# Due times that follow from the next holder of a buffer, a shift by one tensor_reduce, and another order of a split, in a planned attention and MoE kernel on one core

## The chip, the core and the metric

The kernel runs on one core of a Trainium2 chip. Its engines work side by side, each through its own instructions in the order written: TensorE (PE, with PEld for its weight loads), VectorE (DVE), ScalarE (ACT), GpSimd (POOL), and SyncE (SP), which here only issues DMAs. PE writes into PSUM, of which there are 8 banks; DVE and ACT read it, POOL works in SBUF alone. The metric is the device time of one launch in microseconds; less is better.

## The reference

Per batch of 8 and head of 8, with 576 positions and 64 channels, the attention is linear: keys and queries go through an exponential feature map with 128 features. Its output is the input of a dense layer pair (512 to 2048 to 512) with a gate between.

```python
def phi(x):                                   # x scaled by 64 ** -0.25
    proj = np.einsum('bhsd,md->bhsm', x, omega)
    sq = np.sum(x * x, axis=-1, keepdims=True) / 2.0
    h = proj - sq
    h = h - np.max(h, axis=-1, keepdims=True)
    return np.exp(h) / np.sqrt(m)
...
kv = np.einsum('bhsm,bhsd->bhmd', k_p, v)
z = np.sum(k_p, axis=2)
num = np.einsum('bhsm,bhmd->bhsd', q_p, kv)
den = np.einsum('bhsm,bhm->bhs', q_p, z)[..., None] + 1e-06
x = num / den                                 # then (batch, position, head * 64 + channel)
...
h = x @ w_in
sp = np.maximum(h, 0.0) + np.log1p(np.exp(-np.abs(h)))
out = (h * erf(sp)) @ w_out
```

## The kernel before

**Precision.** The large products are made in a fast reduced-precision float form (fp32r). Each operand is split into a high part (a rounded copy) and a low part (the difference), and a product is three matmuls: high by high, high by low, low by high. So a copy ("xhigh", "turnhigh", "high") and a subtraction ("xrest", "turnrest", "rest") stand in front of nearly every matmul.

**Attention.** Two heads make a pair; there are 32 pairs, 4 to a batch (NP). Pairs 0 to 3 (batch 0) go through one by one at the start (`first`, `project_pair`). From pair 4 on, two pairs make a quad (`load`, `project`, `attention`), 14 of them, two to a batch. For keys and for queries of a quad, `project` makes three projections; each fills two PSUM banks (tiles pp), one a pair. For each bank DVE takes the negated maximum over the features (`maximum`, into mx), then `shift` adds the squares, and ACT takes exponentials with that as bias (`exponential`, into f). The squares come from a second layout of q and k (tile un): squared on POOL or ACT, halved twice by POOL additions (`fold`, from 64 to 16 columns a position), and summed by DVE (`sum_squares`, into sq). `shift` runs two scalar_tensor_tensor over the same 6 elements a partition: the squares times half_sq are added to mx and then taken away again, so that mx carries the rounding that the reference has (sq is the same for all features, so it falls out of the exponential but for that rounding). Then `key_values` multiplies exponentials of the keys with v, `turn` transposes those of the queries through PSUM (tiles pt, parts qh and ql), `attend` multiplies both (tiles nd), and a reciprocal and a multiplication on DVE give xs.

**The dense layers.** A batch is 576 positions, two halves of 288. The first layer is done by phase: two phases (ph) a batch, each with 4 granules (fp) of two 128-row blocks. In batches 0 to 2 (PLAIN = 3) a granule is eight plain products (tiles h); from batch 3 on it is seven products of sums and differences of blocks (tiles hS, hA), which takes one product out of eight. Their results are copied or added into hs (names hout and hadd), `chain` runs softplus and erf on ACT for two granules at a time (the activation tables are loaded for it), then the gate (hs times gs, on DVE or POOL), a rounded copy gh and the rest gl. The second layer (`gemm2`, tiles o) of the phase before is done between the granules of this one. Weights are unpacked once in the first two batches by integer operations (wshift, wsign, wtail on tile pw, whigh and wlow on tile w) and then stored and fetched by DMA (wdw, wdcS).

`split` makes the first layer's input parts xh and xl of a batch for c = 0 and 1: lo is the output of pair c, hi that of pair c + 2. In batches 0 to 2 there are two parts, hi (blocks B21, B22) and lo (B11, B12); the first product of every granule reads B11 alone.

**The order.** Nothing is ordered by hand. `build` writes down operations with their possible engines and costs, what they read and write, and for matmuls a planned time. `Plan.order` first gives each operation a due time, from the last to the first: the least of its own planned time and of its successors' due times, less its duration and 0.4. Then it plays the engines forward with these costs: an engine that is idle takes the operation with the earliest due time among those that are ready and whose tiles can be had. Some operations may run on POOL or ACT only if their due time is far enough away. A tile is given to the first operation in the text that uses it, tiles of a stream are given out in the text's order, and their number is limited by SLOTS (buffers of a pool) and CAPS (banks of a stream: 5 for the attention, 3 for the first layer, 2 for the second). Every engine then runs its operations in the order found, whatever the real durations are.

All instructions are issued through one helper, `call`, at line 831, so a profile shows them all at that line and only the tiles tell them apart: mxq and mxk are maxima and shifts, sqq and sqk the sums, unq and unk the squares and folds, fq and fk the exponentials.

Of the kernel before, what the change touches and what calls it, by code (L numbers as in the profile page):

```python
# [14 lines left out]
ALU = mybir.AluOpType  # L15
# [4 lines left out]
P = 128  # L20
# [37 lines left out]

COST = dict(mm=0.132, proj=0.224, turnout=0.33, tr=0.109, kv=0.222, table=1.3)
LAG = {"T": 0.35, "A": 0.35, "V": 0.33, "G": 0.33, "S": 0.3}  # L60
SLOTS = dict(w=8, u=2, un=2, f=2, mx=3, sq=3, v=2, qh=1, ql=1, kh=1, kl=1, rc=2, xs=4, xh=2, xl=2, u2=2,
             hs=4, gs=2, gh=6, gl=6, os=4, ps=8)
CAPS = dict(st=2, wt=2, cv=2, att=5, moe1=3, moe2=2)

# [19 lines left out]

class Op:
    __slots__ = ("opts", "fn", "deps", "succ", "left", "ready", "due", "plan", "uses", "alloc",
                 "name", "id", "half", "set", "macro", "end", "start", "eng", "size")


class Plan:  # L90
# [44 lines left out]
    def order(self, slots, caps):  # L135
# [3 lines left out]
        for o in ops:  # L139
            for d in o.deps:  # L140
                d.succ.append(o)
        for o in reversed(ops):
            due = o.plan if o.plan is not None else math.inf
            dur = min(c for _, c, _ in o.opts)
            for s in o.succ:
                due = min(due, s.due - dur - 0.4)
            o.due = due
        free = {p: list(range(n)) for p, n in slots.items()}
# [187 lines left out]
def build(emit):  # L336
# [50 lines left out]
    def make(u, t):  # L387

        nm = "_".join(str(c) for c in u)
        st = pl.tile("gl", f"st{nm}", [P, HW, 2], I32, "st")  # L390
        pl.op("wload", [("S", 0.1, AHEAD)], lambda e: E.w_load(st, u),
              writes=[(st, 0), (t, "room")], size=P * HW * 8)
        w = pl.tile("gh", f"wt{nm}", [P, HW], I32, "wt")
        pl.op("wbias", [("G", 0.65, WBG), ("A", 0.6, -1e9)], lambda e: E.w_bias(e, st, w),
              reads=[(st, 0)], writes=[(w, 0)])

        p = pl.tile("ps", f"pw{nm}", [P, HW], I32, "pw", PW)
        pl.op("wshift", [("V", 0.6, -1e9)], lambda e: E.w_shift(p, w), reads=[(w, 0)],
              writes=[(p, 0)])
        pl.op("wsign", [("V", 0.6, -1e9)], lambda e: E.w_sign(st, p), reads=[(st, 0), (p, 0)],  # L400
              writes=[(p, 0)])
        pl.op("wtail", [("V", 0.72, -1e9)], lambda e: E.w_tail(st, p), reads=[(st, 0), (p, 0)],
              writes=[(p, 0)])
        parts(t, lambda: p.ap.bitcast(F32).rearrange("p (k c) -> p k c", k=2), [(p, 0)], True)
        store(u, t)
# [82 lines left out]
    def project_pair(n, qk, t0):  # L488
        a = pairs[n]
        u = a["u" + qk]  # L490
        f = a["f" + qk] = pl.tile("gs", f"f{qk}{a['nm']}", [P, NC, P], F32, "f0") \
            if n and qk == "q" else pl.tile("f", f"f{qk}{a['nm']}", [P, NC, P])
        mx = pl.tile("mx", f"mx{qk}{a['nm']}", [P, NC])
        for i in range(3):
            pp = pl.tile("ps", f"pp{qk}{a['nm']}_{i}", [P, 512], F32, "att", early(n))
            pl.op("pair" + qk, [("T", 3 * COST["proj"], -1e9)], lambda e, i=i, pp=pp: E.pair_project(pp, u, qk, i),
                  reads=[(u, ("x", i)), (u, ("s", i))], writes=[(pp, 0)],
                  plan=pair_time(n, t0 + 0.05 * i))
            pl.op("max" + qk, [("V", 0.47, -1e9)], lambda e, i=i, pp=pp: E.maximum(mx, pp, i, None),
                  reads=[(pp, 0)], writes=[(mx, i)])  # L500
            pl.op("exp" + qk, [("A", 0.77, -1e9)], lambda e, i=i, pp=pp: E.exponential(f, mx, pp, i, None),
                  reads=[(pp, 0), (mx, i)], writes=[(f, i)], set="exp")

    def load(m, qk):
        a = quads[m]

        u = a["u" + qk] = pl.tile("u", f"u{qk}{a['nm']}", [P, S2])
        pl.op("load" + qk, [("S", 0.1, 1e9)], lambda e: E.x_load(u, qk, a),
              writes=[(u, 0)], size=P * S2 * 4)
        sq = a["sq" + qk] = pl.tile("sq", f"sq{qk}{a['nm']}", [P, 2, NC])  # L510
        for j, x in enumerate(a["pairs"]):
            un = pl.tile("un", f"un{qk}{x['nm']}", [P, NC * D])
            pl.op("loadn", [("S", 0.1, 1e9)], lambda e, x=x, un=un: E.n_load(un, qk, x),
                  writes=[(un, 0)], size=P * NC * D * 4)
            pl.op("square", [("G", 1.25, -1e9), ("A", 0.75, SQA)],
                  lambda e, un=un: E.square(e, un), reads=[(un, 0)], writes=[(un, 0)])
            pl.op("fold", [("G", 1.05, -1e9)], lambda e, un=un: E.fold(un), reads=[(un, 0)],
                  writes=[(un, 0)])
            pl.op("sumsq", [("V", 0.22, -1e9)], lambda e, un=un, j=j: E.sum_squares(sq, un, j),
                  reads=[(un, 0)], writes=[(sq, j)])  # L520
            if qk == "k":
                v = x["v"] = pl.tile("v", "v" + x["nm"], [P, (NC + 1) * D1])
                pl.op("loadv", [("S", 0.1, 1e9)], lambda e, v=v, x=x: E.v_load(v, x), writes=[(v, 0)],
                      size=P * (NC + 1) * D1 * 4)

    def project(m, qk, t0):
        a = quads[m]
        u, sq = a["u" + qk], a["sq" + qk]
        for j, x in enumerate(a["pairs"]):
            x["f" + qk] = pl.tile("f", f"f{qk}{x['nm']}", [P, NC, P])  # L530
        mx = pl.tile("mx", f"mx{qk}{a['nm']}", [P, 2, NC])
        for i in range(3):
            pps = [pl.tile("ps", f"pp{qk}{x['nm']}_{i}", [P, 512], F32, "att")
                   for x in a["pairs"]]
            pl.op("proj" + qk, [("T", 3 * COST["proj"], -1e9)],
                  lambda e, i=i, pps=pps: E.project(pps, u, i),
                  reads=[(u, 0)], writes=[(pp, 0) for pp in pps] + [(x["f" + qk], "room") for x in a["pairs"]], plan=quad_time(m, t0 + 0.02 * i))
            for j, pp in enumerate(pps):
                pl.op("max" + qk, [("V", 0.47, -1e9)], lambda e, i=i, j=j, pp=pp: E.maximum(mx, pp, i, j),
                      reads=[(pp, 0)], writes=[(mx, (i, j))])  # L540
            pl.op("shift" + qk, [("V", 0.16, -1e9)], lambda e, i=i: E.shift(mx, sq, i),
                  reads=[(sq, j) for j in range(2)] + [(mx, (i, j)) for j in range(2)],
                  writes=[(mx, (i, j)) for j in range(2)])
            for j, (x, pp) in enumerate(zip(a["pairs"], pps)):
                f = x["f" + qk]
                pl.op("exp" + qk, [("A", 0.77, -1e9)],
                      lambda e, i=i, j=j, f=f, pp=pp: E.exponential(f, mx, pp, i, j),
                      reads=[(pp, 0), (mx, (i, j))], writes=[(f, i)], set="exp")
# [57 lines left out]
    def split(b, c):  # L606
# [7 lines left out]
        b11, b12, b21, b22 = half(lo, 0), half(lo, 1), half(hi, 0), half(hi, 1)  # L614
        if b < PLAIN:

            parts = [(0, 2, lambda: hi.ap, b21[1] + b22[1]), (2, 2, lambda: lo.ap, b11[1] + b12[1])]
        else:
            xc = pl.tile("gl", f"xc{b}_{c}", [P, 4, T], F32, "xc", 1)

            def tt(i):
                return lambda: xc.ap[:, i, :], [(xc, i)]
            for i, (x, y) in enumerate(((b12, b11), (b22, tt(0)), (b22, b12), (b21, tt(1)))):
                pl.op("xsum", [("V", 0.4, -1e9), ("G", 0.75, 3.0)],
                      lambda e, x=x, y=y, i=i: E.combine(e, xc.ap[:, i, :], x[0](), y[0](), -1),
                      reads=x[1] + y[1], writes=[(xc, i)])
            parts = [(0, 2, lambda: hi.ap, b21[1] + b22[1]), (2, 1, lambda: lo.ap[:, 0:1], b11[1]),
                     (3, 4, lambda: xc.ap, [(xc, k) for k in range(4)])]
# [185 lines left out]
def tile_attention_moe(ctx: ExitStack, tc: tile.TileContext, qT, kT, qN, kN, vP, omT, w1, w2, out):  # L814
# [66 lines left out]
    class Emit:  # L881
# [81 lines left out]
        def fold(self, un):  # L963
            u = un.ap.rearrange("p (c d) -> p c d", d=D)
            for n in (D // 2, D // 4):
                pool.tensor_add(u[:, :, :n], u[:, :, :n], u[:, :, n:2 * n])

        def sum_squares(self, sq, un, j):
            dve.tensor_reduce(sq.ap[:, j], un.ap.rearrange("p (c d) -> p c d", d=D)[:, :, :D // 4],
                              axis=AX.X, op=ALU.add)  # L970

        def project(self, pps, u, i):
            for c in range(3):
# [3 lines left out]
                              lhsT=u.ap[r, (3 * i + c) * P:(3 * i + c + 1) * P], rhs=(wk if j else wq)[r],  # L977
                              start=True, stop=True)

        def maximum(self, mx, pp, i, j):  # L980
            m = mx.ap if j is None else mx.ap[:, j]
            dve.tensor_reduce(m[:, 3 * i:3 * i + 3],
                              pp.ap[:, :3 * P].rearrange("p (c m) -> p c m", c=3), axis=AX.X,
                              op=ALU.max, negate=True)

        def shift(self, mx, sq, i):
            m, s = (t.ap[:, :, 3 * i:3 * i + 3] for t in (mx, sq))
            for sign in (1.0, -1.0):
                dve.scalar_tensor_tensor(m, s, sign * half_sq, m, op0=ALU.mult, op1=ALU.add)

        def exponential(self, f, mx, pp, i, j):
            m = mx.ap if j is None else mx.ap[:, j]
# [180 lines left out]
```

## Time and profile before

| | |
|---|---|
| median of 3 runs | 1087.71 us (1084.11 to 1089.3) |
| the profiled execution | 1086.37 us, its span 1084.5 us |
| mean granted TensorE clock | 0.989 |
| instructions on PE, DVE, ACT, POOL | 8272, 1515, 1307, 397 |
| DMA | 247.81 MB, mean 229 GB/s |

How to read it: the profiled execution has its own time, and what stands in the rows of the profile adds up to its span. A group row gives line, engine, operation, output and input tiles, shapes and types, the count, then busy time in us and the mean in ns, and after the bar the idle time ahead of them. The chain of work that ended last is followed back from the last instruction, at each step to what released it. Matmuls are pipelined: one is in flight for about 300 ns, and the next starts about 133 ns after it, so a gap shows less in PE's busy share than in its number of matmuls by stage.

### The profile page before, as it was taken

The page shows a single profiled execution, that of the slowest core. Times are in us where ns is not written, and L with a number is a line of the kernel's source. Part 1 is how long each engine was busy: PE and PEld are TensorE (multiplying, and loading weights), DVE is VectorE, ACT ScalarE, POOL GpSimd, SP SyncE. Part 2 cuts the span into 40 slices and gives each one's busy share as a digit, 9 for nine tenths or more (in the row PEclk, how much of TensorE's full clock was granted, in tenths as well). Part 3 has the DMA queues.
Part 4 walks back from the last instruction along what each step waited for, and adds up shares of the span by engine and source line. Part 5 has one row for each costly group of instructions (what it writes and reads, how often), then busy time and mean ns, then how long its engine had stood idle before and what let it go on. Part 6 is the DMA issues. An engine that isn't in the chain of part 4 may idle for free.

```text
span 1084.5 us, 21875 instructions
## 1 busy us (share of the span) xinstructions
PE 1050.5 (97%) x8272; PEld 1021.6 (94%) x8272; DVE 786.1 (72%) x1515; ACT 679.9 (63%) x1307; POOL 443.4 (41%) x397
## 2 busy tenths in 40 slices
PE   7889899999999999899998999989999999999998
PEld 7779898999999999899998999989999999999998
DVE  5989998886597677856788767887678766764451
ACT  8769776866587686656646666475566664464430
POOL 4636436333187485712334233432435312343300
PEclk9999999999999999899998999999999999999999
DMA  8666586687467686577775777767766766667771
GB/s 254 231 223 224 203 288 237 242 284 245 136 218 255 225 306 213 169 260 251 253 232 185 223 257 254 238 206 224 263 222 212 231 198 214 222 230 257 269 231 57
DMA packets 77736, 247.81 MB, mean 229 GB/s; under 512 B 8736, under 2 KB 9120, under 8 KB 77632
## 3 DMA queue, kind: packets, MB, share of 16 engines
q1 hardware_dynamic: 77568, 246.35, 68.0%
q8 instruction: 66, 1.08, 0.4%
q14 instruction: 38, 0.31, 0.1%
q0 software_dynamic: 64, 0.07, 0.0%
HBM read 211.78 MB, written 34.60 MB: 227 GB/s over the span
## 4 chain that ended last, share of the span: by engine, by line
PE 85%; DVE 12%; issue 1%; ACT 1%; DMA 0%; POOL 0%; DVEq 0%; ACTq 0%; POOLq 0%
PE o L831 35%; PE h L831 13%; PE hS L831 11%; PE hA L831 8%; PE kvp L831 5%; PE nd L831 4%; DVE mxq L831 4%; PE ppk L831 4%; PE ppq L831 3%; PE pt L831 2%; DVE pw L831 1%; DVE gl L831 1%; DVE w L831 1%; DVE mxk L831 1%; DVE hs L831 1%
## 5 line engine op out<-in xcount | busy, mean ns | idle before, releaser
L831 PE MATMUL o<-gh,w 128*128 128x288 f32 x2048 | 450.0, 299 | 0.3 <-DVE gl L831 0.3
L831 PEld LDWEIGHTS o<-gh,w 128*128 128x128 f32 x2048 | 340.2, 188 | 4.5 <-DVE gl L831 0.5
L831 PE MATMUL o<-gl,w 128*128 128x288 f32 x1024 | 302.1, 295 | 0.0
L831 PEld LDWEIGHTS o<-gl,w 128*128 128x128 f32 x1024 | 192.8, 188 | 0.1
L831 PE MATMUL h<-xh,w 128*128 128x288 f32 x768 | 176.8, 305 | 4.9 <-DVE w L831 2.0
L831 POOL TENSOR_TENSOR hs<-gs,hs 128x576 f32<-128x576 f32 x62 | 95.6, 1565 | 169.8 <-ACT gs L831 169.8
L831 PE MATMUL hS<-xh,wS 128*128 128x288 f32 x640 | 157.6, 301 | 3.0 <-ACT fq L831 1.7
L831 PEld LDWEIGHTS h<-xh,w 128*128 128x128 f32 x768 | 129.7, 189 | 9.2 <-issue 4.1
L831 POOL TENSOR_TENSOR gl<-hs,gh 128x576 fp32r<-128x576 f32 x64 | 108.5, 1718 | 71.3 <-DVE gh L831 40.2
L831 PE MATMUL hA<-xh,w 128*128 128x288 f32 x480 | 124.7, 304 | 1.8 <-ACT hs L831 1.8
L831 ACT ACT_TABLE_LOAD x92 | 118.0, 1283 | 2.3 <-PEq L1164 0.7
L831 POOL TENSOR_TENSOR unk<-unk 128x144 f32<-128x144 f32 (+2 forms) x73 | 64.0, 887 | 134.7 <-DMA unk<-kN 122.9
L831 PE MATMUL h<-xl,w 128*128 128x288 f32 x384 | 114.0, 297 | 4.1 <-DVE xl L831 4.1
L831 ACT ACTIVATE fq<-ppq,mxq 128x128 f32<-128x128 f32 x288 | 80.2, 385 | 60.0 <-DVE mxq L831 55.0
L831 PEld LDWEIGHTS hS<-xh,wS 128*128 128x128 f32 x640 | 114.5, 193 | 3.4 <-ACT fq L831 1.9
L831 ACT ACTIVATE rc<-nd,eps 64x288 f32<-64x288 f32 x128 | 63.6, 497 | 73.6 <-PE nd L831 61.8
L831 ACT ACTIVATE fk<-ppk,mxk 128x128 f32<-128x128 f32 x288 | 78.7, 390 | 27.3 <-DVE mxk L831 19.0
L831 PE MATMUL hS<-xl,wS 128*128 128x288 f32 x320 | 95.9, 300 | 0.0
L831 PEld LDWEIGHTS hA<-xh,w 128*128 128x128 f32 x480 | 87.2, 192 | 3.2 <-ACT hs L831 2.3
L831 ACT ACTIVATE gs<-hs 128x1152 f32<-128x1152 f32 x64 | 73.1, 1165 | 16.1 <-DVE hs L831 15.7
L831 PEld LDWEIGHTS h<-xl,w 128*128 128x128 f32 x384 | 72.8, 190 | 4.9 <-DVE xl L831 4.3
L831 POOL TENSOR_TENSOR unq<-unq 128x288 f32<-128x288 f32 (+2 forms) x64 | 48.0, 754 | 60.8 <-ACT unq L831 45.6
(104 smaller groups left out, 2131.6 us busy)
## 6 DMA issues: line engine op xcount, KB each, us to landing
w<-wdw SPq DMA_DIRECT2D x184, 512.0 KB, 4.5
wS<-wdcS SPq DMA_DIRECT2D x80, 512.0 KB, 4.1
st<-w SPq DMA_DIRECT2D x32, 512.0 KB, 4.6
wdw<-w SPq DMA_DIRECT2D x32, 512.0 KB, 3.9
v<-vP SPq DMA_DIRECT2D x32, 325.0 KB, 3.4
w<-wdw SPq DMA_DIRECT2D x40, 256.0 KB, 3.8
out<-os SPq DMA_DIRECT2D x32, 288.0 KB, 3.8
wdcS<-cS SPq DMA_DIRECT2D x16, 512.0 KB, 5.0
```

The source lines that it names most:

```text
L831: return tc.keep_in_program_order(method(*args, **kwargs))
```

## The change

Four things are changed.

1. *Due times.* For each tile of a stream with a limit, the tile that comes that many places later in the stream (which can be given out only when this one is free) has a first user, the heir. Every operation that uses the tile and stands ahead of the heir in the text, and isn't one of its predecessors, is now due before the heir as well.
2. *The shift.* The sq tile has three columns for a position: the sum of squares, the negated sum, and the negated maximum. `fold` scales the squares by half_sq on POOL with a third instruction (128x144). `sum_squares` runs twice for each half, once negated. `maximum` writes its result into the third column, and `shift` is one tensor_reduce that adds the three columns into mx.
3. *Buffers and costs.* mx and sq have 2 buffers and no longer 3; the planner's costs of wshift and wsign are 0.7 and not 0.6, of fold 1.3 and not 1.05, of the shift 0.17 and not 0.16.
4. *The split.* In batches 0 to 2 the part of pairs 0 and 1 (lo) stands in the text ahead of that of pairs 2 and 3 (hi).

```diff
-SLOTS = dict(w=8, u=2, un=2, f=2, mx=3, sq=3, ...
+SLOTS = dict(w=8, u=2, un=2, f=2, mx=2, sq=2, ...
...
+        for o in ops:
+            o.later = []
+        for stream in self.streams.values():
+            for n, t in enumerate(stream):
+                room = t.cap or caps.get(t.stream) or (slots[t.pool] if t.pool == t.stream else 0)
+                if room and n + room < len(stream):
+                    heir = stream[n + room].users[0]
+                    for o in t.users:
+                        if o.id < heir.id and o not in heir.deps:
+                            o.later.append(heir)
         for o in reversed(ops):
             due = o.plan if o.plan is not None else math.inf
             dur = min(c for _, c, _ in o.opts)
-            for s in o.succ:
+            for s in o.succ + o.later:
                 due = min(due, s.due - dur - 0.4)
...
-        pl.op("wshift", [("V", 0.6, -1e9)], ...
+        pl.op("wshift", [("V", 0.7, -1e9)], ...
-        pl.op("wsign", [("V", 0.6, -1e9)], ...
+        pl.op("wsign", [("V", 0.7, -1e9)], ...
...
-        sq = a["sq" + qk] = pl.tile("sq", f"sq{qk}{a['nm']}", [P, 2, NC])
+        sq = a["sq" + qk] = pl.tile("sq", f"sq{qk}{a['nm']}", [P, 2, NC, 3])
...
-            parts = [(0, 2, lambda: hi.ap, b21[1] + b22[1]), (2, 2, lambda: lo.ap, b11[1] + b12[1])]
+            parts = [(2, 2, lambda: lo.ap, b11[1] + b12[1]), (0, 2, lambda: hi.ap, b21[1] + b22[1])]
...
             for n in (D // 2, D // 4):
                 pool.tensor_add(u[:, :, :n], u[:, :, :n], u[:, :, n:2 * n])
-
-        def sum_squares(self, sq, un, j):
-            dve.tensor_reduce(sq.ap[:, j], un.ap.rearrange("p (c d) -> p c d", d=D)[:, :, :D // 4],
-                              axis=AX.X, op=ALU.add)
+            u = u[:, :, :D // 4]
+            pool.tensor_scalar(u, u, half_sq, 0.0, op0=ALU.mult, op1=ALU.add)
+
+        def sum_squares(self, sq, un, j, x):
+            dve.tensor_reduce(sq.ap[:, j, :, x], un.ap.rearrange("p (c d) -> p c d", d=D)[:, :, :D // 4],
+                              axis=AX.X, op=ALU.add, negate=bool(x))
...
         def shift(self, mx, sq, i):
-            m, s = (t.ap[:, :, 3 * i:3 * i + 3] for t in (mx, sq))
-            for sign in (1.0, -1.0):
-                dve.scalar_tensor_tensor(m, s, sign * half_sq, m, op0=ALU.mult, op1=ALU.add)
+            dve.tensor_reduce(mx.ap[:, :, 3 * i:3 * i + 3], sq.ap[:, :, 3 * i:3 * i + 3], axis=AX.X, op=ALU.add)
```

More of the change, by code (lines that the diff above doesn't have):

```diff
@@ L60 @@
 LAG = {"T": 0.35, "A": 0.35, "V": 0.33, "G": 0.33, "S": 0.3}
-SLOTS = dict(w=8, u=2, un=2, f=2, mx=3, sq=3, v=2, qh=1, ql=1, kh=1, kl=1, rc=2, xs=4, xh=2, xl=2, u2=2,
+SLOTS = dict(w=8, u=2, un=2, f=2, mx=2, sq=2, v=2, qh=1, ql=1, kh=1, kl=1, rc=2, xs=4, xh=2, xl=2, u2=2,
              hs=4, gs=2, gh=6, gl=6, os=4, ps=8)
@@ L86 @@
     __slots__ = ("opts", "fn", "deps", "succ", "left", "ready", "due", "plan", "uses", "alloc",
-                 "name", "id", "half", "set", "macro", "end", "start", "eng", "size")
+                 "name", "id", "later", "half", "set", "macro", "end", "start", "eng", "size")
 class Plan:
@@ L397, in make @@
         p = pl.tile("ps", f"pw{nm}", [P, HW], I32, "pw", PW)
-        pl.op("wshift", [("V", 0.6, -1e9)], lambda e: E.w_shift(p, w), reads=[(w, 0)],
+        pl.op("wshift", [("V", 0.7, -1e9)], lambda e: E.w_shift(p, w), reads=[(w, 0)],
               writes=[(p, 0)])
-        pl.op("wsign", [("V", 0.6, -1e9)], lambda e: E.w_sign(st, p), reads=[(st, 0), (p, 0)],
+        pl.op("wsign", [("V", 0.7, -1e9)], lambda e: E.w_sign(st, p), reads=[(st, 0), (p, 0)],
               writes=[(p, 0)])
@@ L498, in project_pair @@
                   plan=pair_time(n, t0 + 0.05 * i))
-            pl.op("max" + qk, [("V", 0.47, -1e9)], lambda e, i=i, pp=pp: E.maximum(mx, pp, i, None),
+            pl.op("max" + qk, [("V", 0.47, -1e9)], lambda e, i=i, pp=pp: E.maximum(mx.ap, pp, i),
                   reads=[(pp, 0)], writes=[(mx, i)])
@@ L516, in load @@
                   lambda e, un=un: E.square(e, un), reads=[(un, 0)], writes=[(un, 0)])
-            pl.op("fold", [("G", 1.05, -1e9)], lambda e, un=un: E.fold(un), reads=[(un, 0)],
+            pl.op("fold", [("G", 1.3, -1e9)], lambda e, un=un: E.fold(un), reads=[(un, 0)],
                   writes=[(un, 0)])
-            pl.op("sumsq", [("V", 0.22, -1e9)], lambda e, un=un, j=j: E.sum_squares(sq, un, j),
-                  reads=[(un, 0)], writes=[(sq, j)])
+            for x_ in range(2):
+                pl.op("sumsq", [("V", 0.22, -1e9)], lambda e, un=un, j=j, x_=x_: E.sum_squares(sq, un, j, x_),
+                      reads=[(un, 0)], writes=[(sq, (j, x_))])
             if qk == "k":
@@ L538, in project @@
             for j, pp in enumerate(pps):
[L539 to L542, printed above, removed]
+                pl.op("max" + qk, [("V", 0.47, -1e9)], lambda e, i=i, j=j, pp=pp: E.maximum(sq.ap[:, j, :, 2], pp, i),
+                      reads=[(pp, 0)], writes=[(sq, (j, (2, i)))])
+            pl.op("shift" + qk, [("V", 0.17, -1e9)], lambda e, i=i: E.shift(mx, sq, i),
+                  reads=[(sq, (j, x)) for j in range(2) for x in (0, 1, (2, i))],
                   writes=[(mx, (i, j)) for j in range(2)])
@@ L978, in project, with maximum @@
                               start=True, stop=True)
-        def maximum(self, mx, pp, i, j):
-            m = mx.ap if j is None else mx.ap[:, j]
+        def maximum(self, m, pp, i):
             dve.tensor_reduce(m[:, 3 * i:3 * i + 3],
```

## The prediction, made before the result was known

> **What bounds the kernel now.** I read the page first, then the windows by stage, then PE's own waits, then the chain of work around the longest of them.
>
> ```profile
> span 1084.5 us, 21875 instructions
> PE 1050.5 (97%) x8272; PEld 1021.6 (94%) x8272; DVE 786.1 (72%) x1515; ACT 679.9 (63%) x1307; POOL 443.4 (41%) x397
> PE 85%; DVE 12%; issue 1%; ACT 1%; DMA 0%; POOL 0%; DVEq 0%; ACTq 0%; POOLq 0%
> ```
>
> PE carries 85% of the chain that ended last, DVE 12%: a tensor-bound kernel in which VectorE now and then decides. A PE that is busy 97% of the time isn't proof of full speed, so I looked at how many matmuls it gets through by stage.
>
> ```profile
> core 0: us, PE busy (x) PEld busy (x) DVE busy (x) ACT busy (x) POOL busy (x), PEclk, DMA share, GB/s
> 55.00:130.00 75.00, 68.48 (x514) 63.97 (x515) 67.81 (x126) 59.97 (x121) 36.51 (x37) 0.98 0.62 214
> 200.00:430.00 230.00, 230.00 (x1868) 225.74 (x1866) 170.11 (x314) 159.18 (x313) 117.06 (x101) 1.00 0.70 240
> 570.00:600.00 30.00, 26.70 (x198) 25.69 (x198) 23.94 (x42) 20.88 (x37) 13.90 (x14) 0.89 0.61 196
> ```
>
> Between 200 and 430 us PE has no gap and runs 8.1 matmuls per us: nothing can be gained there. Between 570 and 600 it runs 6.6 per us, at a granted clock of 0.89. The time to be had lies in a few such places, and PE's waits name them.
>
> ```profile
> PE pt L831 <- DVE ql L831: 4.7, 2, 2.4
> PE h L831 <- DVE xl L831: 4.1, 1, 4.1
> PE h L831 <- DVE w L831: 2.0, 3, 1.6
> PE h L831 <- issue: 1.9, 1, 1.9
> PE hA L831 <- ACT hs L831: 1.8, 2, 0.9
> PE hS L831 <- ACT fq L831: 1.7, 1, 1.7
> PE hS L831 <- DVE ql L831: 1.3, 1, 1.3
> PE ppq L831 <- ACT fq L831: 0.8, 1, 0.8
> ...
> PE o L831 <- DVE gl L831: 0.3, 1, 0.3
> ```
>
> Three places after 430 us carry most of them: 447 to 452 (fq 1.7 and 0.8), 584 to 588 and 715 to 719 (ql 2.4 and hs 0.9 at each). The 1.3 lies at 846. What decides there is in the chain, here a piece behind the first place and then the run that ends in the second:
>
> ```profile
> 452.49 3.25 PE hS L831 x12
> ...
> 579.77 1.54 DVE gh L831
> 581.67 2.14 DVE gl L831
> ...
> 584.78 1.31 DVE mxq L831
> 586.12 1.32 DVE mxq L831
> ...
> 588.11 0.47 DVE ql L831
> 588.72 0.87 PE pt L831 x3
> ...
> 590.32 1.44 PE hS L831 x6
> ...
> 595.39 1.59 PE hS L831 x12
> ...
> 598.17 0.79 PE hS L831 x6
> ```
>
> From 579.77 to 588.59 DVE works through without a pause, PE waits for its last piece, ql, which frees a PSUM bank for the transpose pt. The two pieces of 1.31 and 1.32 us are the two scalar_tensor_tensor of one shift, each on 6 elements a partition. And the price doesn't end with the wait: six matmuls at 590.32 take 1.44 us, the same six at 598.17 take 0.79; twelve at 452.49 take 3.25, twelve at 595.39 take 1.59. Adding up all slow groups behind each place in this way gives 2.7 us at 588, 1.7 at 720, 2.6 at 452 and 0.3 at 847. With the waits (3.3, 3.3, 2.5 and 1.3) these four places cost 6.0 + 5.0 + 5.1 + 1.6 = **17.7 us**, of which 10.4 are waits.
>
> The Trainium skill ("TensorE: Matmul & The Clock Gate", "What's actually happening") has the array go cold after an idle window of about 3.4 us. By that, waits of 3.3 us in two pieces needn't cost any clock, and the four places would be worth 10.4 us; the slow groups say otherwise.
>
> **The change, part by part: the shift.** It removes two scalar_tensor_tensor for each of 84 shifts and puts one tensor_reduce in their place; sums of squares are made twice, once negated.
>
> ```profile
> L831 DVE SCALAR_TENSOR_TENSOR mxq<-sqq,mxq 128x6 f32<-128x6 f32 x84 | 43.2, 514 | 2.7
> L831 DVE SCALAR_TENSOR_TENSOR mxk<-sqk,mxk 128x6 f32<-128x6 f32 x84 | 14.8, 188 | 2.2
> L831 DVE SCALAR_TENSOR_TENSOR mxq<-sqq,mxq x84: 155/169/1382, 71.6 to 905.5; 128x6 f32<-128x6 f32 x84
> L831 DVE TENSOR_REDUCE sqq<-unq x28: 291/294/308, 35.1 to 819.8; 128x9 f32<-128x144 f32 x28
> L831 DVE TENSOR_REDUCE mxq<-ppq x96: 540/548/560, 10.3 to 904.7; 128x3 f32<-128x384 f32 x96
> 584.64 2.78 POOL L831 TENSOR_TENSOR gl<-hs,gh 128x576 fp32r<-128x576 f32 x2 [2.04 <-ACT gh L831]
> ```
>
> The old instruction has a median of 169 ns and a maximum of 1382. The POOL row shows what it waits for: POOL's two halves of gl run from 584.64 to 587.4, 1.4 us each, and the two slow instructions end with them. The tensor_reduce over the same squares, read from SBUF alone, never exceeds 308 ns in 28. So the new shift isn't held by POOL. Its length: from 144 to 384 elements a reduce grows from 294 to 548 ns, 1.06 ns an element, so 18 elements come to 294 - 126 x 1.06 = 160 ns (ends 155, the quickest old one, and 294). DVE loses 43.2 + 14.8 = 58.0 us, gains 84 x 0.16 = 13.4 and 56 x 0.294 = 16.5 for the second sums: 28 us less in all, 17 by the upper end. On the path, a pair before each of two places (engine, operation, then the count):
>
> ```profile
> 440.00 2.21 DVE L831 SCALAR_TENSOR_TENSOR mxq<-sqq,mxq 128x6 f32<-128x6 f32 x2
> ...
> 573.39 1.77 DVE L831 SCALAR_TENSOR_TENSOR mxq<-sqq,mxq 128x6 f32<-128x6 f32 x2
> ```
>
> Ahead of 588 the pairs at 573.39 and 584.78 take 1.77 + 2.63 = 4.4 us and would take 0.32: 4.1 us off a run of DVE work whose end PE awaits for 3.3. The pair at 440.00 gives 2.0 towards the 2.5 waited from 447 on. With the order of instructions as it is, nearly all four places would close: -17.7 at most. But the due rule sorts the instructions there anew, and no row shows the new order. I take two thirds, **-12**; ends 0 and -17.7.
>
> The Trainium skill speaks against this part ("VectorE: DVE Perf Modes", "Rules for kernel authors"): it calls tensor_reduce the slowest DVE operation on a hot path. Taken so, a new shift would cost no less than an unheld old pair, 0.34 us, and DVE's saving would be 13 us instead of 28, and the saving ahead of 588 would be 3.7 instead of 4.1, still above the wait: the sum would stay.
>
> **What the shift adds elsewhere.** POOL gets 56 scalings of 128x144 in the fold.
>
> ```profile
> L831 POOL TENSOR_TENSOR unk<-unk 128x144 f32<-128x144 f32 x28 | 16.2, 578 | 2.2
> L831 POOL TENSOR_SCALAR xh<-xs 128x288 fp32r<-128x288 f32 x5 | 2.7, 547 | 56.7 <-PE hS L831 56.5 <-PE h L831 0.2
> ```
>
> Between the two-input row of 578 ns and what the one-input row of 288 elements leaves for half as many, say 0.3 to 0.58, I take 0.46: 26 us on an engine that is 41% busy. Behind a fold on POOL stand gates and rests; before a shift stands the sum, whose last instance starts at 819.8 while the last shift starts at 905.5. That lead is the cover, for the longer fold, the second sum and the drop from 3 to 2 sq buffers (a sum must now wait until the shifts of two tiles earlier are done): 0. mx with 2 buffers: the tiles alternate between k and q, their exponentials are done a third of a 61 us phase before the next use, 0. If the cover goes, exponentials and with them the transposes are late.
>
> **The split order.** In the first three batches xh is allocated by the first user in the text, which was the half made of pairs 2 and 3. PE's largest single wait shows it:
>
> ```profile
> 54.01 1.55 POOL L831 TENSOR_TENSOR xl<-xs,xh 128x288 fp32r<-128x288 f32 x2 [4.27 <-ACT xh L831]
> 57.36 0.75 DVE L831 TENSOR_TENSOR xl<-xs,xh 128x576 fp32r<-128x576 f32 x1
> 61.01 4.23 PE h L831 x27
> ```
>
> PE waits 4.1 us for an xl that DVE runs from 57.36 to 58.11, behind maxima and shifts, though it needs only pair 1, finished long before. Split first, that half is there, and PE waits for the other half instead: its xh comes just ahead of the xl that POOL ends at 55.56. That is 2.55 us, and the slow groups behind it (27 matmuls in 4.23 us, where 27 at the rate of 12 in 1.59 take 3.6) leave some 0.7 more in this row. I take **-3**; ends 0 and -4.8. In batches 1 and 2 PE has no wait for a split: 0.
>
> **The due rule.** By the planner's own figures a phase is 4 x 90 x 0.132 + 13.8 = 61.3 us. A query projection's first exponential was due before its transpose, 0.15 x 61.3 x 1.1 = 10.1 us on, less 1.2. Of five attention banks it holds the first; the sixth tile belongs to the third projection, 2.7 us on, so it is now due at about 1.5, 7.4 us earlier. Copies out of the three MoE banks were due with the softplus, tens of us on, and are now due before the third product after them, some 3 us on. So maxima, shifts, exponentials, bank copies and ql move ahead of gates, casts and rests, which is what stood in front of ql at 579 to 583. What PE waits for is freed sooner; gates are late next. ACT may switch tables more often:
>
> ```profile
> L831 ACT ACT_TABLE_LOAD x92 | 118.0, 1283 | 2.3 <-PEq L1164 0.7
> ```
>
> 32 chains with three sets each allow 96, so at most 4 x 1.28 = 5 us on an engine at 63%: 0. Beyond what stands above I give the rule nothing in the steady part, and **-1** of the 3.9 us that PE waits for w and for no visible cause ("issue") between 110 and 170 us (ends 0 and -3.9). The new costs of 0.7 for wshift and wsign only move the plan: 0.
>
> **Sum.** -12 - 3 - 1 = -16 against the profiled execution's 1086.4 us (span 1084.5 and 1.9 around it): 1070.4. The median of the runs is 1.3 above it: **1072**.
>
> **The rivals.** (a) Everything closes: 17.7 + 4.8 + 3.9 = 26 off, and the 1.3 added: 1061; 1055 if the early stages, where DVE is 90% busy (67.8 of 75 us), also shorten by 6 us with fewer held instructions. For it: the same run of DVE work stands in front of each place. Against: new orders make new waits. (b) Waits change place: DVE, crowded at each query projection, meets the next held instruction (gl at 581.67 took 2.14 us), and the gain is 0 to 5: about 1085. (c) Slower, by one mechanism: exponentials and maxima, now due first, push the gate, cast and rest of a chain so far back that the second GEMM waits for gl, once in a quad. This trace has 0.3 us of PE waiting for gl in all, so there is some margin, of unknown size. One such wait costs what 584 to 588 costs, 6.0; three eat the gain, four give slower by over 0.5%, and five of the 14 quads would give 1072 + 30 = 1102. (d) The slow groups don't come of the waits and stay where they are: then two thirds of 10.4 us go at the four places instead of two thirds of 17.7, and the time is 1072 + 5 = 1077. Against it: at three of the places they begin with the first matmul after the wait. The clock-gate page of the Trainium skill, as told above, would have it so.
>
> **How the numbers follow.** My forecast (1064 to 1076) 0.45; (a) 0.14; (d), or another gain of only 6 to 11 us, 0.12; (b) 0.16; (c) 0.13. Runs of this kernel spread by 0.5%, and that is about what tells a change from none: faster is below 1082.3, slower above 1093.1. Faster 0.71, same 0.16, slower 0.13. The range from 1055 to 1093 leaves out (c) and a little on the other side.
>
> **What would show it.** Shift reduces of 128x6<-128x18 near 0.16 us with a maximum under 0.35; DVE busy 17 to 28 us lower; POOL 26 higher; the wait of PE h for DVE xl near 54 us gone or below 2; no run of DVE pieces longer than 10 us on the chain behind a query projection; PE hS <- ACT fq, PE pt <- DVE ql and the half-clock groups gone. I'm wrong if PE o waits for gl or gh by several us in total, if new waits of PE for ACT fq appear, or if the early stages, where DVE is the fullest, grow longer than 200 us took before.

## The result, and the profile after

The changed kernel takes **1059.93 us** (median, 1058.16 to 1061.49), against 1086.99 for the kernel before in the same comparison: a ratio of 0.9752, 95% interval 0.9722 to 0.9782, or 27 us. The forecast was 1072, with 1061 as the time of rival (a): the measured time lies inside the stated range of 1055 to 1093, but below the 1064 to 1076 that the forecast gave itself. The page of the changed kernel, its first lines and its chain:

```profile
span 1058.4 us, 21952 instructions
PE 1042.0 (98%) x8272; PEld 1014.2 (96%) x8272; DVE 752.0 (71%) x1488; ACT 681.9 (64%) x1302; POOL 458.8 (43%) x458
PE 92%; DVE 3%; DMA 2%; POOL 1%; issue 1%; SPq 1%; ACT 0%; DVEq 0%; POOLq 0%; ACTq 0%
```

The same 8272 matmuls, 26 us sooner; DVE's share of the chain has gone from 12% to 3%. Where the time went is told by the number of matmuls that PE starts in fixed stretches (us from the start, PE, PEld, DVE, ACT, POOL busy, then the granted clock). Of the kernel before:

```profile
0.00:130.00 130.00, 113.55 (x832) 104.23 (x833) 109.04 (x213) 104.13 (x240) 67.32 (x79) 0.99 0.68 225
430.00:1040.00 610.00, 598.02 (x4732) 586.30 (x4731) 431.18 (x853) 359.02 (x629) 225.39 (x184) 0.99 0.70 230
```

Of the changed kernel:

```profile
0.00:130.00 130.00, 120.52 (x931) 113.12 (x932) 111.87 (x228) 111.58 (x263) 74.53 (x94) 0.99 0.72 238
130.00:200.00 70.00, 67.46 (x530) 64.61 (x529) 62.48 (x123) 53.55 (x105) 39.03 (x44) 1.00 0.82 280
200.00:430.00 230.00, 230.00 (x1855) 223.73 (x1854) 158.03 (x291) 158.37 (x309) 127.90 (x122) 1.00 0.67 230
430.00:1040.00 610.00, 609.23 (x4852) 598.19 (x4851) 416.88 (x843) 358.38 (x626) 217.36 (x200) 1.00 0.70 235
```

A matmul count alone misleads here, because the kinds differ in length. The chain of the changed kernel shows what each kind takes, one after the other:

```profile
550.82 0.84 PE kvp L842 x8
...
562.32 0.87 PE ppq L842 x12
...
566.58 0.33 PE pt L842 x3
...
572.42 0.81 PE hA L842 x6
...
573.56 0.40 PE nd L842 x3
```

That is 0.133 us for a long one (o, h, hS, hA and nd), 0.07 for a projection, 0.11 for a transposition and 0.105 for a kvp. With the counts of each kind, from the window view of its tile, the matmuls that the changed kernel starts more or fewer than the kernel before become work, an estimate from these rows:

| stretch, us | long | projections | pt | kvp | all | work, us |
|---|---|---|---|---|---|---|
| 0 to 130 | 18 | 36 | 9 | 36 | 99 | 9.7 |
| 130 to 200 | 61 | -36 | 0 | -36 | -11 | 1.8 |
| 200 to 430 | -38 | 12 | -9 | 22 | -13 | -2.9 |
| 430 to 1040 | 157 | -12 | 0 | -25 | 120 | 17.4 |

The sum is 26.0 us, and the spans are 26.1 apart. (For every kernel below, the same sum also meets the difference of the spans within 0.3 us.) So there are two gains: 8.6 us by 430 us, nearly all of it in the first 130, and 17.4 us after 430. Between 200 and 430 neither kernel shows a gap on PE, as the prediction read it, yet the changed one does some 3 us less work there; why is left open.

PE's waits from 200 to 1040 us, all that the view gives:

```profile
PE hA L842 <- DVE u L842: 0.4, 1, 0.4
PE o L842 <- DMA w<-wdw: 0.3, 1, 0.3
```

The four places with 10.4 us of waits are gone. What DVE does now at a query projection, in order of time (start, length, engine, operation):

```profile
563.22 1.02 DVE L842 TENSOR_REDUCE sqq<-ppq 128x3 f32<-128x384 f32 x2
564.28 0.17 DVE L842 TENSOR_REDUCE mxq<-sqq 128x6 f32<-128x18 f32 x1
...
566.94 0.56 DVE L842 CAST qh<-pt 128x384 fp32r<-128x384 f32 x1 [0.27 <-PE pt L842]
567.42 0.45 DVE L842 COPY hs<-hA 128x288 f32<-128x288 f32 x1
567.78 0.55 DVE L842 TENSOR_TENSOR ql<-pt,qh 128x384 fp32r<-128x384 f32 x1
...
569.30 1.35 DVE L842 TENSOR_TENSOR hs<-gs,hs 128x1152 f32<-128x1152 f32 x1
```

Two things differ from 579 to 588 us before. The shift is one instruction of 0.17 us, where two took 2.63. And qh, ql and the bank copies (hs from hA) come ahead of the gate, where the cast and the rest of the gate (1.54 and 2.14) stood ahead of ql. The trace can't say which of the two closed the places, since either could. The experiments take them apart.

### The profile page after: what moved, and what is told of

Its sections match the earlier page's. It is cut to its first block, busy times and chain, and to the rows that moved or that the text cites. A ratio compares the mean times of both kernels' runs of the same rounds, so it can differ in the third digit from the quotient of the medians.

```text
span 1058.4 us, 21952 instructions
## 1 busy us (share of the span) xinstructions
PE 1042.0 (98%) x8272; PEld 1014.2 (96%) x8272; DVE 752.0 (71%) x1488; ACT 681.9 (64%) x1302; POOL 458.8 (43%) x458
## 4 chain that ended last, share of the span: by engine, by line
PE 92%; DVE 3%; DMA 2%; POOL 1%; issue 1%; SPq 1%; ACT 0%; DVEq 0%; POOLq 0%; ACTq 0%
PE o L842 39%; PE h L842 14%; PE hS L842 12%; PE hA L842 9%; PE kvp L842 5%; PE nd L842 4%; PE ppq L842 3%; PE ppk L842 3%; PE pt L842 2%; DMA uq<-qT 1%; DVE pw L842 1%; SPq L842 1%; POOL unq L842 0%; POOL uq L842 0%; POOL unk L842 0%
## 5 line engine op out<-in xcount | busy, mean ns | idle before, releaser
L842 PE MATMUL o<-gh,w 128*128 128x288 f32 x2048 | 458.7, 301 | 2.8 <-DVE w L842 2.5
L842 PE MATMUL h<-xh,w 128*128 128x288 f32 x768 | 173.9, 303 | 0.3 <-ACT xh L842 0.3
L842 POOL TENSOR_TENSOR gl<-hs,gh 128x576 fp32r<-128x576 f32 x60 | 100.0, 1690 | 61.2 <-ACT gh L842 30.9
L842 PE MATMUL hA<-xh,w 128*128 128x288 f32 x480 | 122.1, 298 | 0.4 <-DVE u L842 0.4
L842 PEld LDWEIGHTS hS<-xh,wS 128*128 128x128 f32 x640 | 112.1, 188 | 0.3 <-DVE u L842 0.3
L842 POOL TENSOR_TENSOR unk<-unk 128x288 f32<-128x288 f32 (+2 forms) x72 | 58.5, 816 | 55.0 <-ACT unk L842 27.3
```

Of the source, the lines that this page charges most:

```text
L842: return tc.keep_in_program_order(method(*args, **kwargs))
```

## Instruction or order

**The order of before, with the new instructions in the old places.** The planner sees the old operations and costs; only what they issue is changed, and mx has two real buffers and no longer three (with a third sq buffer there is no room for three columns in it). By its code the sum that stays in the column is the positive one, so what it leaves out is the negated sum, not the positive.

```diff
-        sq = ... [P, 2, NC])
+        sq = ... [P, 2, NC, 2])
...
+            u = u[:, :, :D // 4]
+            pool.tensor_scalar(u, u, half_sq, 0.0, op0=ALU.mult, op1=ALU.add)
-            dve.tensor_reduce(sq.ap[:, j], ...)
+            for x in range(2):
+                dve.tensor_reduce(sq.ap[:, j, :, 0], ..., negate=not x)
-            for sign in (1.0, -1.0):
-                dve.scalar_tensor_tensor(m, s, sign * half_sq, m, op0=ALU.mult, op1=ALU.add)
+            dve.tensor_reduce(mx.ap[:, :, 3 * i:3 * i + 3], sq.ap[:, :, 3 * i:3 * i + 3], axis=AX.X, op=ALU.add)
```

> The order of the kernel before, to the instruction, with the new instructions put in the old places: fold scales, sums are made twice, one tensor_reduce of two columns is the shift. It leaves out the positive sum of squares in the shift, for want of SBUF (the third sq buffer), so its output isn't the reference's. Theory I (the instruction: a shift that POOL doesn't hold closes the four places at 447, 584, 715 and 846 us): 12 to 18 us faster than before, 1069 to 1075; these four waits of PE gone, the first 130 us as before. Theory O (the order: the due rule closes them, because ql, maxima and copies come ahead of gates): at most 4 us faster, 1083 to 1088, the places still there, only shorter by what the shifts took less.

1078.72 us, ratio 0.9919 (0.9897 to 0.9940): 9 us, between the two theories. The profiled execution took 1080.43, above the median, so its windows show 6 us of gain and not 9. Its windows and its waits of PE from 200 to 1040:

```profile
0.00:130.00 130.00, 112.82 (x809) 103.18 (x810) 105.47 (x210) 100.86 (x228) 68.55 (x88) 0.95 0.66 219
430.00:1040.00 610.00, 603.02 (x4817) 592.67 (x4817) 418.54 (x843) 364.20 (x644) 237.43 (x209) 1.00 0.71 235
```

```profile
PE hS L831 <- ACT fq L831: 4.2, 1, 4.2
PE hA L831 <- ACT hs L831: 1.7, 2, 0.9
```

After 430 us it gains 85 matmuls, 11.0 us of work: the waits of pt and hS for ql are gone (4.7 and 1.3 before). In the first 130 us it loses 23, all of them long, 3 us, and by 430 us it is 5.3 us behind. The second sums, the scalings and the lost buffer of mx can each have a part in that, and so can the execution that was profiled; no run takes them apart. And one place, the first, is worse than before: 4.2 us of waiting for exponentials, at 454. The chain that ends there runs through POOL and no longer through DVE:

```profile
444.52 0.76 POOL L831 TENSOR_SCALAR unk<-unk 128x144 f32<-128x144 f32 x1
445.36 2.50 POOL L831 TENSOR_TENSOR unk<-unk 128x288 f32<-128x288 f32 x2
447.95 0.31 POOL L831 TENSOR_SCALAR unk<-unk 128x144 f32<-128x144 f32 x1
448.34 7.79 POOL L831 TENSOR_TENSOR hs<-gs,hs 128x576 f32<-128x576 f32 x4
```

Two folds with their scalings stand in front of four halves of a gate, ACT's cast of it waits for the gate, and the exponentials that PE needs stand behind that cast on ACT. From 442.74 to 448.26 the folds take 5.5 us, the scalings 1.07 of them; in the kernel before, the additions alone took 3.4. So the wait taken off DVE came back by way of POOL, because in the old order the cast stands ahead of the exponentials.

**The order of the changed kernel, with the old instructions.**

```diff
-            u = u[:, :, :D // 4]
-            pool.tensor_scalar(u, u, half_sq, 0.0, op0=ALU.mult, op1=ALU.add)
...
+            if x:
+                return
-            dve.tensor_reduce(mx.ap[:, :, 3 * i:3 * i + 3], sq.ap[:, :, 3 * i:3 * i + 3], axis=AX.X, op=ALU.add)
+            dve.scalar_tensor_tensor(m, s[:, :, :, 0], half_sq, s[:, :, :, 2], op0=ALU.mult, op1=ALU.add)
+            dve.scalar_tensor_tensor(m, s[:, :, :, 0], -half_sq, m, op0=ALU.mult, op1=ALU.add)
```

> The order of the changed kernel with the old instructions in the new places: two scalar_tensor_tensor as the shift, no scaling in the fold, one sum for each half. Theory I: the stalls come back, within 6 us of the kernel before: 1080 to 1088. Theory O: at most 4 us slower than the changed kernel, 1059 to 1064, with held shifts on DVE (means of 0.3 us and more) that PE doesn't notice.

1069.28 us, ratio 0.9838 (0.9799 to 0.9878): 18 us. Its windows, then its waits of PE from 200 to 1040, then its shift instructions (ns, least, median, most):

```profile
0.00:130.00 130.00, 119.22 (x921) 112.00 (x921) 112.69 (x226) 109.58 (x258) 71.13 (x82) 0.99 0.71 234
130.00:200.00 70.00, 65.95 (x491) 62.13 (x490) 61.74 (x115) 49.22 (x104) 28.89 (x32) 0.95 0.73 255
430.00:1040.00 610.00, 607.37 (x4838) 595.64 (x4838) 432.26 (x868) 365.94 (x634) 211.35 (x180) 1.00 0.70 236
```

```profile
PE hA L842 <- ACT fq L842: 1.7, 1, 1.7
PE o L842 <- DVE os L842: 0.7, 1, 0.7
PE h L842 <- ACT fq L842: 0.4, 1, 0.4
PE o L842 <- DMA w<-wdw: 0.3, 1, 0.3
```

```profile
L842 DVE SCALAR_TENSOR_TENSOR mxq<-sqq x42: 154/341/1385, 68.7 to 888.1; 128x6 f32<-128x6 f32 x42
```

The shifts are held as before, up to 1385 ns, and PE hardly waits after 200 us (3.1 us in all): with ql and the copies ahead of gates, DVE's lost time seems to fall on work that nobody awaits. The work ahead of the kernel before, reckoned as above from each one's profiled execution:

| | by 430 us | after 430 us | sum | spans apart |
|---|---|---|---|---|
| old order, new instructions | -5.3 | 11.0 | 5.7 | 5.8 |
| new order, old instructions | 1.4 | 14.3 | 15.8 | 15.8 |
| both (the changed kernel) | 8.6 | 17.4 | 26.0 | 26.1 |

After 430 us instruction and order close the same places: 11.0 and 14.3 alone, 17.4 together, and neither theory is the whole. At the start it is otherwise. The order alone is 8.4 us ahead at 130 us, but loses 3.3 of it by 200 (491 matmuls, 530 with the new instructions) and 3.7 more by 430; the instruction alone is behind; only both together keep a gain. That 9 and 18 add up to 27 is therefore no sign of two independent effects: late they overlap, and early, in these executions, each needs the other. (The plan of the new order reckons with the new instructions' costs, so with the old ones its early part isn't what was planned.)

## The parts, planned anew

Each of these is sorted anew by the planner, so it shows what a part is worth as one would write it, with the luck of its order. The diffs are hunks of the change shown above, put in or left out.

**The due rule alone** (the two hunks with `later`, on the kernel before).

> The kernel before with the due rule alone (old instructions, old split, 3 buffers, old costs). Theory I: 0 to 6 us faster, 1081 to 1088, with gains in the first 130 us only. Theory O: 15 to 22 us faster, 1065 to 1072, the places after 430 us closed.

1083.25 us, ratio 0.9965 (0.9939 to 0.9992): 4 us, as Theory I had it in size, but not in place: its profiled execution is 7.3 us of work behind by 430 us and 8.5 ahead after. PE's first waits over the whole span:

```profile
PE ppk L841 <- DVE wk L841: 4.8, 1, 4.8
PE o L841 <- DVE os L841: 4.3, 5, 1.7
PE nd L841 <- DVE qh L841: 2.8, 3, 1.2
PE ppq L841 <- DVE os L841: 2.0, 1, 2.0
```

The waits for ql have gone, and waits for os, the copies of the second layer out of its two banks, have come in their place (all of the 4.3 us after 430). That held shifts make DVE late for these copies is likely, but not shown. The first row is the start of the kernel, 4.7 to 5.0 us in every version.

**The new shift alone**, planned as such.

```diff
-            parts = [(2, 2, lambda: lo.ap, ...), (0, 2, lambda: hi.ap, ...)]
+            parts = [(0, 2, lambda: hi.ap, ...), (2, 2, lambda: lo.ap, ...)]
...
-        pl.op("wshift", [("V", 0.7, ...
+        pl.op("wshift", [("V", 0.6, ...
...
-            for s in o.succ + o.later:
+            for s in o.succ:
```

(against the changed kernel; wsign likewise)

> The kernel before with the new shift alone, planned as such (two sq and mx buffers, its new costs; old due rule, old split, old costs of wshift and wsign). Theory I: 12 to 18 us faster, 1069 to 1075. Theory O: at most 4 us faster, 1083 to 1088; since it is planned anew, the places of the stalls may move.

1072.95 us, ratio 0.9877 (0.9838 to 0.9916): 13 us, what Theory I expected. All of it comes late: 791 matmuls in the first 130 us (832 before), 4850 after 430 (4732), or 2.6 us of work lost by 430 and 15.6 gained after.

**The split alone** (its one line, on the kernel before).

> The kernel before with the half of pairs 0 and 1 split first, nothing else. Theory S (the split's order makes the early gain, by itself): 4 to 11 us faster, all of it before 130 us; 1077 to 1084. Theory X (the early gain needs the parts together, since the whole order is made anew by each): within 3 us of before, 1085 to 1091.

1085.01 us, ratio 0.9983 (0.9966 to 1.0000): at most 4 us, and not clear of nothing. PE's waits between 40 and 70 us, in this kernel:

```profile
PE ppk L831 <- DVE xs L831: 1.8, 2, 1.4
PE ppq L831 <- DVE xs L831: 0.4, 1, 0.4
PE ppk L831 <- ACT fk L831: 0.2, 1, 0.2
```

The wait of 4.1 us for xl is gone, as it should be. PE then runs into xs, the next thing that DVE has to deliver: 843 matmuls by 130 us instead of 832, which is no gain in work: it has 64 long ones fewer, and 75 short ones more.

**All but the shift** (due rule, split, costs), and **all but the due rule**:

> The changed kernel without the new shift: due rule, split and the new costs of wshift and wsign on the kernel before (old instructions, 3 buffers). The order of the changed kernel with the old instructions took 1069.3. Theory S: due rule (5 us by itself) and split (4 to 11) add up: 1073 to 1080. Theory X: far from the sum, below 1070 or above 1083.

> The changed kernel with the old due rule. Theory I (the instruction closes the late places): 1060 to 1066, the late places closed, since the due rule by itself was worth 5 us. Theory O (the due rule closes what the instruction leaves): 1067 to 1075, with waits of PE after 430 us.

Without the shift 1078.12 us, ratio 0.9908 (0.9880 to 0.9937): 10 us, where the due rule and the split alone give 6 together; again 4.3 us of waits for os, and in work 2.4 us ahead by 430 and 10.5 after. Without the due rule 1064.22, ratio 0.9789 (0.9764 to 0.9814). That is 4 us behind the changed kernel by the medians, with intervals that just overlap. Its waits of PE show what the rule closes: three of up to 0.9 us for hs after 430 us; and by 430 us it is 3.6 us of work ahead of the kernel before, where the changed kernel is 8.6. (The profiled execution took 1067.27, 3 us above the median.)

**All but the split**, **all but the new costs of wshift and wsign**, and **the shift with these costs alone**:

> The changed kernel with the old order of the split. Theory S: 4 to 11 us slower than the changed kernel, 1064 to 1071, with a wait of PE for xl or xh between 45 and 60 us. Theory X: a difference of any size in any place; if within 2 us, 1058 to 1062, the split is worth nothing here.

> The changed kernel with the planner's old costs of wshift and wsign (0.6). Theory C (with costs that match the measured 0.69 us the plan of the first 130 us holds on the chip, and the early gain of 11 us rests on it): 5 to 10 us slower than the changed kernel, 1065 to 1070, all before 130 us. Theory D (the due rule makes the early gain): within 2 us, 1058 to 1062.

> The new shift and the new costs of wshift and wsign, with the old due rule and the old split. The shift alone took 1073.0, with costs and split 1064.2. Theory C: the costs make that difference, 1062 to 1067. Theory S (the split makes it): 1071 to 1075.

1060.71 us without the split, ratio 0.9755 (0.9738 to 0.9771): nothing. 1062.75 with the old costs, 0.9779 (0.9757 to 0.9802): 3 us by the medians, not clear. 1067.82 for shift and costs, 0.9821 (0.9802 to 0.9840), against 0.9877 for the shift alone: some 6 us, with intervals that just touch, and 852 matmuls by 130 us instead of 791. So Theory S, that the split makes the early gain, fails. Theory C is half right: the costs help where the due rule is absent and hardly where it is there. Matmuls started by 130 us and the work ahead of the kernel before at 430 us, from the profiled execution of each:

| kernel | due rule | split | new costs | matmuls by 130 us | work ahead at 430, us | median us |
|---|---|---|---|---|---|---|
| shift alone | no | no | no | 791 | -2.6 | 1072.95 |
| shift and costs | no | no | yes | 852 | 4.1 | 1067.82 |
| all but the due rule | no | yes | yes | 855 | 3.6 | 1064.22 |
| all but the costs | yes | yes | no | 910 | 7.1 | 1062.75 |
| all but the split | yes | no | yes | 913 | 8.0 | 1060.71 |
| changed kernel | yes | yes | yes | 931 | 8.6 | 1059.93 |

All six have the new shift. Two steps stand out, 5 to 7 us of work each: the new costs beside the shift alone, and the due rule beside all the rest. Even these aren't clear, since executions of the kernel before differ by 5 us, and the smaller steps can't be told from nothing.

## What the new shift costs, and a version without it

**The changed kernel's order with one sum** (it leaves out the scaling and the negated sum):

```diff
-            u = u[:, :, :D // 4]
-            pool.tensor_scalar(u, u, half_sq, 0.0, op0=ALU.mult, op1=ALU.add)
...
+            if x:
+                return
-            dve.tensor_reduce(..., sq.ap[:, :, 3 * i:3 * i + 3], axis=AX.X, op=ALU.add)
+            dve.tensor_reduce(..., sq.ap[:, :, 3 * i:3 * i + 3, 0:3:2], axis=AX.X, op=ALU.add)
```

> The changed kernel, in its order, without what the new shift adds: no scaling on POOL, no second sum on DVE; the shift adds two columns with a stride. It leaves out the negated sum, so its output isn't the reference's. If the additions cost on the path what the old order with new operations lost in the first 160 us (5 us): 1054 to 1057. If they are hidden: 1058 to 1061.

1057.78 us, ratio 0.9729 (0.9710 to 0.9748). By the medians 2 us better than the changed kernel, intervals overlapping; 948 matmuls by 130 us against 931, and 4845 after 430 us against 4852. So the additions may cost some 2 us, or nothing; these runs can't tell.

**No squares at all** in the quads, nor the 56 loads for them:

```diff
-        sq = a["sq" + qk] = pl.tile("sq", ...)
...
-            un = pl.tile("un", ...)
-            ... loadn, square, fold, sumsq
...
-                pl.op("max" + qk, ..., E.maximum(sq.ap[:, j, :, 2], pp, i), ... writes=[(sq, (j, (2, i)))])
-            pl.op("shift" + qk, ...)
+                pl.op("max" + qk, ..., E.maximum(mx.ap[:, j], pp, i), ... writes=[(mx, (i, j))])
```

> The changed kernel without squares, folds, sums and shift in the quads (they are the same for all features of a position, so they fall out of the quotient; the rounding that the shift carries is left out), and so without 56 loads of 288 KB. If PE's remaining waits come of DVE's and POOL's load: 1048 to 1055. If PE is at its limit but for the start: 1055 to 1060, all of the gain before 160 us.

1052.25 us, ratio 0.9673 (0.9653 to 0.9693): the fastest, and better than both kernels. Its page and its windows:

```profile
PE 1039.4 (99%) x8272; PEld 1013.0 (96%) x8272; DVE 702.2 (67%) x1282; ACT 665.5 (63%) x1274; POOL 341.3 (32%) x272
```

```profile
0.00:130.00 130.00, 121.38 (x934) 114.01 (x935) 108.06 (x199) 111.67 (x266) 49.21 (x54) 0.99 0.65 218
130.00:200.00 70.00, 70.00 (x557) 67.88 (x556) 61.22 (x105) 50.39 (x102) 23.71 (x21) 1.00 0.72 252
```

POOL has 117 us less to do and DVE 50, and the loads are gone too, so this run can't say which of the three frees PE. PE gets 8 us by the medians. In work it is 3.7 us ahead of the changed kernel between 130 and 200 us, 0.6 elsewhere by 430 and 2.5 after. In size this is the first expectation, in place half the second: the larger part of the gain lies before PE is at its pace. It gives up the rounding that the shift carries, so it isn't the same arithmetic to the last bit.

## Why the prediction came out as it did

- **The places.** Right. Four places after 430 us with 17.7 us were named, and after 430 us 17.4 us of work were gained. The half-clock groups went with the waits: the granted clock is 1.00 in every window of the changed kernel after 130 us. Rival (d), that they are none of the waits' doing, has nothing left for it.
- **The instruction.** Right in kind and size: 160 ns were worked out, 172 measured, and never held:

```profile
L842 DVE TENSOR_REDUCE mxq<-sqq x42: 154/172/175, 68.3 to 877.8; 128x6 f32<-128x18 f32 x42
L842 POOL TENSOR_SCALAR unk<-unk x28: 303/311/1352, 19.5 to 762.5; 128x144 f32<-128x144 f32 x28
```

  The second row is the scaling on POOL, sized at 0.46 us and 0.31 in the median. DVE is busy 34 us less (786.1 to 752.0), more than the 17 to 28 forecast; POOL 15 us more (443.4 to 458.8), not 26. The Trainium skill ("VectorE: DVE Perf Modes", "Rules for kernel authors") calls tensor_reduce the slowest DVE operation; here one takes 0.172 us, as long as one unheld old instruction (0.169), where two were needed.
- **On the path, -12.** This term was too small by 5.4 us: the places closed whole. It had been cut to two thirds because a new order could make new waits, and in the new order none came (0.7 us of waits after 200 us). In the unchanged order, where the instruction alone gains 11.0 us, a place did stay open, because POOL became late.
- **"What the shift adds elsewhere", 0.** Not settled. In the old order 23 matmuls are lost in the first 130 us, with the other candidates named above; with one sum in the new order 17 come back, 2 us by the medians with intervals that overlap.
- **The split, -3.** The wait did go, and the next thing that was late, xs, took its place. No run shows more than 4 us for it, and in the finished kernel it is worth nothing that can be told.
- **The due rule, -1, and the new costs, 0.** Both probably too small. Without the due rule the changed kernel is 4 us slower by the medians; the costs are worth some 6 us beside the shift alone; neither is clear of its intervals. With the split these were the forecast's early gains, 4 us in all, and 8.6 came by 430 us. The forecast looked for them in two of PE's waits (the 4.1 for xl, and 1 of the 3.9). But the view of the first 130 us sums to 15.8 us of waits before, many of them small, and to 9.1 after, of which these rows are the most:

```profile
PE ppk L842 <- DVE wk L842: 5.0, 1, 5.0
...
PE nd L842 <- DVE qh L842: 1.9, 1, 1.9
PE ppq L842 <- DVE xs L842: 1.1, 1, 1.1
```

- **The sum.** The 5.4 us late and 4.6 early are what the forecast (1070.4 for the profiled execution, which took 1060.85) fell short by. No single part carries it: most of the late places is closed by the instruction or by the order alone, and the early gain comes with both together.
- **The rivals.** (a), everything closes, 1061, is what happened, at a chance of 0.14. Of its 17.7 us late, 17.4 were measured. Its 8.7 us early come near the 8.6 in part by luck: the waits for w, which it counted, are still there (2.5 us between 130 and 200), and others that it didn't count are gone. (b), waits change place, is what each part does alone: os for ql under the due rule, xs for xl under the split, POOL for DVE under the instruction. (c) didn't come: the view shows no wait of PE for gl after 200 us.

What stays open: which of the plan's inputs makes how much of the early order. The single steps of 0 to 6 us overlap or just touch in their intervals, every part sorts the whole order anew, and the work by stage comes from one profiled execution of each kernel.

## What to carry to other kernels

Where an order is planned, a stall has two cures, a shorter instruction ahead of it and a better place for the awaited one; test each with the other held fixed, and look at each stage by itself: here the two overlapped late and needed each other early, and totals of 9, 18 and 27 us hid both. A part that removes a wait is worth what the next late thing leaves: find that next thing before you count. When you compare stages of two orders, count the instructions started by kind, each at its own length, beside the named waits: at 8.1 per us, the plain counts of 99 and 120 would have given 12 and 15 us where the work was 9 and 17.

## What the runs showed of the hardware

- A DVE instruction of 6 elements with two SBUF inputs takes 0.17 us, or up to 1.38 beside POOL: in the kernel before, 44 of the 168 took over 0.25 us, and each of these ended 16 to 28 ns after a POOL instruction. A tensor_reduce with a single input of 18 elements takes 0.154 to 0.175, also in the 31 of 84 cases that lie wholly inside a running two-input POOL instruction. POOL can be late too: its scaling at 579.95 us in the changed kernel, 0.31 us in the median, took 1.35 beside a DVE subtraction with two SBUF inputs that ran from 579.78 to 581.13.
- In the kernel before, waits of 0.9 and 2.4 us with six matmuls between them, from 584.3 to 588.7 us, were followed by half the rate of matmuls. These are the window that takes in the end of the second wait, and one 10 us on (PE's count and the granted clock):

```profile
588.00:595.00 7.00, 6.28 (x29) 6.31 (x30) 4.55 (x12) 2.31 (x7) 1.29 (x2) 0.54 0.61 184
598.00:605.00 7.00, 7.00 (x56) 7.00 (x55) 3.90 (x10) 6.62 (x7) 0.00 (x0) 1.00 0.88 267
```

  29 matmuls at a clock of 0.54 and then 56 at 1.00. The Trainium skill ("TensorE: Matmul & The Clock Gate", "What's actually happening") asks for an idle window of about 3.4 us; here 3.3 in two pieces were enough.
